# A planned transformer block on one core: all loads on one queue inside the plan, and the norm of segment 2 turned on TensorE

## The chip, the cores and the metric

The kernel runs on one core of a Trainium2 chip. The metric is device time in microseconds (us). A core has five engines that run side by side, each with a queue of its own in a fixed order: TensorE (PE), VectorE (DVE), ScalarE (ACT), GpSimd (POOL) and SyncE (SP). SP and ACT also issue DMA transfers[...].

## The reference

`x` has 2048 rows of 448, all in bf16. A vector `c` gives six modulation vectors through `silu(c) @ w_mod`.

```python
sa, ca, ga, sb, cb, gb = six rows of silu(c) @ w_mod
h = layernorm(x) * (1 + ca) + sa
x = x + ga * attention(h)          # 16 heads of 28, 4 segments of 512
h = layernorm(x) * (1 + cb) + sb
x = x + gb * ((sigmoid(h @ w_gate) * (h @ w_up)) @ w_down)   # inner width 1792
```

Attention is causal within a segment, with `g = sigmoid(beta)` for each head mixing in a memory of the earlier segments: `o = g * phi(q) M / (phi(q) z + 1e-6) + (1 - g) * softmax(q k) v`, and after each segment `M += phi(k)^T v`, `z += sum phi(k)`, with `phi(t) = t + 1` above zero and `exp(t)` below.

## The kernel before

**A plan, then the program.** The function builds a graph: `add` (L150) makes a node of each piece of work, with the engines that can do it, a duration, what it depends on and which buffers it takes. `Graph.run` (L209) plays this graph in planned time: each engine takes the ready node with the highest rank plus priority, where a choice of engine depends on `COST`, and PE stays with one kind of matmul for a bonus `STAY`. The order that comes out is written into each engine's queue. Small priorities for nearly all nodes stand in a table, `PRM`, by kind of work ("lg" logits, "ex" exponentials, "gu" gate and up, "mem" memory and so on). Planned times only decide the order; on the chip each engine goes through its queue in that order and waits where data is late.

**What is computed where.** A segment is 512 rows, four tiles of 128. For each segment:

- `ln1` (L792): statistics of a tile (L562, L563, DVE), 1/sigma (L569, L570, POOL), normalised tile `xn` (L575, DVE). Then `xn` has to be turned so that features lie on partitions (`hT`), and scale and shift are applied per partition. There are two ways. `turned` (L755) does it on PE: 32 transposes (L765) into four PSUM banks, then seven evacuations with scale and shift (L785 on DVE, L787 on ACT). The other way is four DMA transposes issued by SP (`transposed`, L708 and L710), then four modulations in place (`modulated`, L713; L720 ACT, L722 DVE or POOL), and two DMAs that copy halves of partitions (L727, L730). The tuple `PE_LN1` (L350) names the segments from the first on that take the PE way; segment 0 always does.
- `proj` (L813): q and k (L825) and v (L837) matmuls, evacuated by L808 (ACT) or L810 (DVE).
- `attention` (L887): logits (L906), exponentials (L920, L926, ACT), masks (L933 POOL, L936 DVE), values (`unit`, L953; L961), then small DVE work.
- `memory` (L856): phi of k (L850, L851, L853) gives `pq`, which a DMA transpose on SP (L861) turns to `pk`; the matmuls (L869) then add to the memory.
- `wo_ln2` (L1018): output projection (L1028), residual (L1031), second norm, turned by DMA for all segments.
- `ffn` (L1043): 14 chunks of gate and up (L1050), tanh (L1055, ACT), product (L1057, DVE), then the down projection (L1069), the residual (L1076) and the store (L1078).

All of PE's program order is one queue: a memory matmul that waits for its `pk` holds back every matmul placed behind it.

**The loads.** `load` (L438) makes a node of 600 ns on the issuing engine and a second node without work, released at a time `land` that is written by hand for each load. The plan takes the data to be there at that time. The transfers' sizes play no part, though `moved` (L171) and the queue clocks `self.ring` (L220) are in the code: no node passes `move`. A DMA transpose counts as landed 1240 ns after its issue (`lag`). The loads alternate: SP has `c`, tiles 0 and 2 of x, half of the first modulation weights, k weights, half of v and then most of the rest; ACT has tiles 1 and 3, the other half of the modulation weights, q weights, two tiles of segment 1, half of v, and both gate weights, the last behind segment 2's x. Their priorities `first(i)` (L468) follow the order of the source. The x of segment 3 (L673) waits for the warm-up matmuls (L657), which read its place. `scaled` (L699) multiplies each of the 14 chunks of down weights by `gb`; every chunk waits for all loads of down weights.

DMAs on SP share eight completion counters in turn, so a DMA waits until the eighth before it has landed.

```python
def load(eng, dst, src, land, deps=(), prio=0, use=(), take=()):
...
    n = add(eng, 600, fn, deps, prio=prio, use=use, take=take)
    return add("SP", 0, None, [n], prio=prio, release=land * 1000)
...
W_d = [scaled(wd_sb, k, 1, [n_gb, *l_wd]) for k in range(NFC)]
```

Of the kernel before, what the change touches and what calls it, by code (L numbers as in the profile page):

```python
# [13 lines left out]
P = 128  # L14
# [4 lines left out]
LAND = 1600  # L19
BACKLOG = 1500  # L20
INF = float("inf")
ALONE, SHARED = 215.0, 145.0

PRM = {
    "ws": (-1026557, -380405, -315274, -238661, -361567, 90434, -31526, -713703, -423901, -193540, 139595, 62071,
        -178802, 31458, -500017, -126626, -750922, -813085),
    "pj": (338550, 1240916, 411576, 1061850, 1037161, 271405, 605973, 841448, 517860, 274333, 556557, 602204, 435753,
        945539, 369290, 776037, 909231, 192884, 459168, 322714, 406428, 656300, 245224, -363562, -225384, -786626,
        -223846, -820139, -425637, -906561, -1127628, 367112, 198381, 481751, 18329, 758012, 1032656, 828671, 241536,
        -108484, 239872, -119492, 199009, -281816, 301267),  # L30
    "ev": (311356, 765090, 171478, 487831, 1411031, 758695, 745068, 1515510, 1532854, 1405197, 1664306, 1094315,
        -114560, 174326, 479074, -88836, 462561, 261587, 915583, 89350, 382455, 177146, -444871, 297079, -491875,
        -222386, -1021935, -1117245, -944968, -693323, -712045, 156181, -647130, -819253, -453667, -850771, 249532,
        470376, 69329, -181432, -477828, -275085, -331069, -936587, -284845, -325847, 8756, 195150),
    "ln1": (1117654, 765673, 978450, 1341531, 982229, 811634, 236741, 912635, 1047582, 168013, 717920, 598649, 902832,
        1278552, 1261149, 970655, 1361456, 978155, 746622, 409077, 386546, 264763, 501671, 55814, 137348, 244764,
        505320, 215607, 544820, 1205735, 581882, 756242, 340737, 854593, 668848, 969330, 981049, 750772, 802670,
        616966, 465825, 1027566, -527936, -40158, 551712, -96720, 326911, 50091, 727172, 256793, 1038149, -131304,
        434030, 588604, 808073, 645081, 880576, 1080680, 723034, 524922, 692343),
    "lg": (674902, 123695, 561301, 319397, 645874, 437068, 206227, 207503, 422863, 143555, 1405617, 879359, 868834,  # L40
        1242253, 807012, 1506890, 954487, 1724581, 1713292, 1378785, 1485021, 676801, 444818, 973580, 812305, 1769904,
        2086894, 2555751, 2316080, 3140941, 1912861, 1735115, 1765623, 1581983, 2149029, 1748985, 1870959, 2367380,
        1278299, 893760),
    "ex": (1061159, 1477133, 1739179, 1359130, 1621557, 896827, 896235, 802625, 1177741, 2146583, 883183, 786963,
        642153, 1848965, 1700468, 722258, 746990, 660348, 192999, 773605, 1217384, 1475898, 1178507, 1397622, 765939,
        582409, 211476, 196729, 217511, 138682, 267517, 735941, 973892, 608471, 890967, 881450, 1005686, 512596,
        717021, 1327086),
    "mask": (1520615, 1413694, 1279386, 2003105, 1818148, 1973568, 1670422, 2469718, 1732752, 2449207, 2306151,
        2540750, 2040307, 1834958, 2435499, 2237411, 1296838, 1432044, 1532957, 1218967, 1170467, 1705939, 960787,
        1030549, 742853, 1076535, 994933, 1817637, 1621845, 1174157, 1217475, 1346691, 104169, 318120, 14934, 89176,  # L50
        -135831, -486501, 272715, 347507, 378087, 1065118, -303844, 343822, 80679, -50290, -474178, -736840, -1557112,
        -1468651, -1261640, -1303527, -1057597, -1141215, -1062730, -1763005, -1399556, -1166602, -1202915, -1688388,
        -1993199, -1843840, -2304918, -2315887),
    "pv": (2080873, 874575, 1009647, 487727, 296192, 1097797, 857940, 480897, 821614, 1153384, 660808, 137298, 190263,
        216055, 377708, 836178),
    "t": (-44324, -21055, -29785, 323641, 1006485, 278236, 167569, 856460, 297038, 195779, 68830, 895442, 358856,
        455925, 730160, 976669, 660644, 556043, 354807, 376622, -321978, 157415, 864924, -137626, -13313, 290080,
        372271, 1258384, 607806, 1462055, 819535, 1127215, 1768030, 2069621, 812504, 1337124, 1749731, 1387778,
        1413501, 2478807, 2325887, 2562860, 1857402, 2208536, 2212781, 2183598, 2015299, 2167715, 598865, 1226474,
        520219, 548995, 636417, 958748, 460961, 506437, -81660, 79568, 966288, -7132, 344038, 633991, 435718, 626174,  # L60
        1339615, 932678, 1119918, 1241109, 965629, 1222800, 104675, 343254, 539346, 531196, 62549, -113912, 833029,
        813798, 408749, 253522, 741436, 740463, 767728, -6116, 485147, -287524, 95432, 156825, -74345, -203303,
        510344, 357634, 156656, -14091, -167467, 107793, -226537, -76689, 44264, -219803, 678406, 634786, 1038779,
        344264),
    "mem": (-185723, 115729, 59349, 101126, -27425, -125584, 150803, 226014, 77645, 95180, -386111, -12099, 159007,
        105014, -92900, 142903, -177695, -219275, 81591, 169437, 244125, -176994, 373563, 312329, 79103, 228949,
        339820, 303405, -105541, -4612, 38191, -535059, -581776, -270138, -483070, -69831, -419676, -163082, -119046,
        -338816, -647557, 205497, 121315, 18139, 1524, -617796, -58030, -28127, -466040, -307104, -92751, -96592,
        -453196, 116369, -188149, 204464, -251426, -250860, 458314, 392143, -371182, 9140, -889615, 673864, 781648,
        -240091, -16361, 399549, 206298, 47390, -303080, 370641, 102082, 458188, -136876, 332910, -790048, -209712,  # L70
        -550212, -485136, -241698, -185202, -576074, -371146),
    "wo": (2112408, 2093060, 2305611, 2035838, 435162, 1036304, 475885, 771414, 630045, 1079320, 1559197, 1122679,
        356509, 300181, -12581, -595879),
    "ln2": (1499349, 1911242, 2271005, 2227074, 1714614, 2066603, 2313937, 2292776, 2160756, 2211288, 2128912,
        2208921, 2494562, 2645243, 2017403, 2025602, 1875862, 2683834, 1770257, 1753157, 2151609, 1620369, 2211622,
        2044129, 2041746, 2243335, 561335, 696447, 969893, 837539, 590753, 252632, 1124331, 450641, 499934, 955682,
        653646, 594227, 565736, 929045, 685791, 706665, 954319, 503582, 1307997, 222097, 532639, 560506, 656449,
        953930, 865631, 662258, 747483, 724968, 974588, 920306, 1228076, 582694, 1487720, 1328136, 1048415, 948930,
        534287, 911788, 951510, 652778, 1847938, 1107426, 1049821, 668310, 1069501, 1109227, 1555135, 1261802,
        1318123, 2035851, 1417382, 2225008, -161015, 1031266, 1417875, 378351, 786858, 1716123, 1229095, 701535,  # L80
        769515, 857183, 963575, 521701, 391767, 1206676, 711474, 1156260, 880842, 923158, 606379, -147848, 528713,
        1255901, 447053, 717115, 872039, 365082),
    "gu": (982010, 1055412, 1188460, 953099, 705622, 838949, 1541378, 1520265, 1523761, 1634808, 949038, 1205958,
        832621, 1228260, 1311640, 290384, 877513, 536067, 481700, 502669, 400060, 885562, 705837, 515193, 270457,
        679260, 95423, 516376, 427829, 422138, -404887, -519560, 2520, -144327, 77521, -126967, 242348, -370325,
        -1248825, -108870, 41043, 293765, 182463, 2284, 520519, -709033, -533470, -308110, -919140, -1297023, -156020,
        -736908, -410023, -242206, -1116015, -657782, 472002, -58716, -30694, 26640),
    "tanh": (1916179, 1874612, 1112957, 1758741, 1844683, 2214238, 1662134, 1941088, 2051357, 2010608, 1710485,
        1638932, 1374883, 1611235, 657651, 874309, 137725, 129323, 697315, 1542469, 318956, 660289, 1212104, 668024,
        499705, 2746, 275789, -204972, -1127385, -525042, -1317983, -778761, -1052030, -953142, -1111022, -1480677,  # L90
        -247404, -561265, -648359, 340744, -871092, -628201, -599047, -491261, -651988, -197450, -489600, -495926,
# [18 lines left out]
STAY = 151782  # L110
# [1011 lines left out]
```

## Time and profile before

| | |
|---|---|
| median of 3 runs | 272.6 us (270.68 to 273.43) |
| the profiled execution | 274.04 us |
| its span, first to last instruction | 272.3 us |
| mean granted clock of TensorE | 0.937 |
| PE busy | 244.9 us (90%) |
| DVE busy | 194.0 us (71%) |
| ACT busy | 152.0 us (56%) |
| POOL busy | 48.9 us (18%) |
| read from HBM | 11.07 MB |

The profile's page cuts the span into 40 slices of 6.8 us, with the busy share of each engine in tenths, the clock granted to TensorE in tenths of the full one (PEclk) and the rate of the DMA engines (GB/s). Groups of instructions are named by line of the kernel, engine, and output and input by the program's names. A wait is written "engine line <- what released it: total us, times, longest". Times in a timeline count from the start of the span. Issue of a DMA is shown on its engine's queue (SPq).

### The profile page before, as it was taken

The page shows a single profiled execution, that of the slowest core. Times are in us where ns is not written, and L with a number is a line of the kernel's source. Part 1 is how long each engine was busy: PE and PEld are TensorE (multiplying, and loading weights), DVE is VectorE, ACT ScalarE, POOL GpSimd, SP SyncE. Part 2 cuts the span into 40 slices and gives each one's busy share as a digit, 9 for nine tenths or more (in the row PEclk, how much of TensorE's full clock was granted, in tenths as well). Part 3 has the DMA queues.
Part 4 walks back from the last instruction along what each step waited for, and adds up shares of the span by engine and source line. Part 5 has one row for each costly group of instructions (what it writes and reads, how often), then busy time and mean ns, then how long its engine had stood idle before and what let it go on. Part 6 is the DMA issues. An engine that isn't in the chain of part 4 may idle for free. (4 is left out here: it accounts for less than half of the span.)

```text
span 272.3 us, 5953 instructions
## 1 busy us (share of the span) xinstructions
PE 244.9 (90%) x2365; PEld 110.9 (41%) x2365; DVE 194.0 (71%) x484; ACT 152.0 (56%) x188; POOL 48.9 (18%) x104
## 2 busy tenths in 40 slices
PE   8799898187598798999998899989999999999995
PEld 3544653023243234443433543533444444445442
DVE  4579976296999979598898999759978653433431
ACT  2227979077979956466898589486621142112310
POOL 5204130041052001103501215303003110000000
PEclk9869899559999569999999999999999999999999
DMA  7999999930527510001035200240101320010001
GB/s 188 198 220 212 243 251 275 163 90 0 79 51 99 125 22 19 2 0 23 19 59 142 57 2 0 55 65 31 34 2 34 77 70 0 19 51 0 4 27 41
DMA packets 32103, 20.75 MB, mean 76 GB/s; under 512 B 20491, under 2 KB 30412, under 8 KB 32076
## 3 DMA queue, kind: packets, MB, share of 16 engines
q1 hardware_dynamic: 29868, 17.11, 30.4%
q10 hardware_dynamic: 2208, 3.27, 5.3%
q8 instruction: 18, 0.29, 0.5%
q14 instruction: 9, 0.07, 0.1%
HBM read 11.07 MB, written 1.84 MB: 47 GB/s over the span
## 5 line engine op out<-in xcount | busy, mean ns | idle before, releaser
L1050 PE MATMUL ps<-hT,wgu 64*128 64x512 bf16 x784 | 94.5, 385 | 2.3 <-DVE aT L810 0.9
L1055 ACT ACTIVATE tt<-ps 128x512 f32<-128x512 f32 x56 | 33.4, 597 | 66.6 <-PE ps L1050 65.8
L920 ACT ACTIVATE pT<-ps 128x2048 bf16<-128x2048 f32 x32 | 60.2, 1881 | 13.6 <-PE ps L906 11.9
L1057 DVE SCALAR_TENSOR_TENSOR fT<-tt,ps 128x512 bf16<-128x512 f32 x56 | 38.1, 682 | 31.7 <-ACT tt L1055 31.6
L1050 PEld LDWEIGHTS <-wgu 64*128 64x128 bf16 x784 | 40.2, 95 | 49.3 <-issue 13.1
L1069 PE MATMUL ps<-wd_sb,fT 128*128 128x448 bf16 x224 | 45.8, 353 | 0.2 <-DVE kT L810 0.2
L933 POOL TENSOR_SCALAR_AFFINE_SELECT pT<-pT 128x512 bf16<-128x512 bf16 x29 | 18.1, 635 | 73.1 <-DVE O L1009 21.1
L1069 PEld LDWEIGHTS <-fT 128*128 128x128 bf16 x224 | 20.4, 98 | 22.6 <-issue 5.7
L825 PE MATMUL ps<-hT,wqk 64*128 64x512 bf16 x224 | 28.8, 392 | 0.4 <-DVE x_sb L1031 0.4
L562 DVE BATCH_NORM_STATS2 st<-x_sb 128x6 f32<-128x448 bf16 x32 | 19.6, 614 | 3.0 <-DMA x_sb<-in_A_x_dram 2.5
L906 PE MATMUL ps<-qT,kT 28*128 28x512 bf16 (+3 forms) x256 | 17.0, 319 | 3.2 <-ACT pT L920 3.0
L825 PEld LDWEIGHTS <-wqk 64*128 64x128 bf16 x224 | 12.5, 97 | 14.0 <-issue 3.0
L926 ACT ACTIVATE pT<-ps 128x2048 bf16<-128x2048 f32 x8 | 15.0, 1875 | 5.2 <-PE ps L906 5.2
L1076 DVE TENSOR_TENSOR ot<-ps,x_sb 128x448 bf16<-128x448 f32 x16 | 9.8, 614 | 9.0 <-PE ps L1069 8.7
L570 POOL TENSOR_TENSOR rs<-rs,mhalf 128x1 f32<-128x1 f32 (+1 forms) x26 | 15.8, 609 | 2.2
L1028 PE MATMUL ps<-wo_sb,oT 128*128 128x448 bf16 x64 | 13.5, 353 | 2.5 <-ACT pT L920 1.5
L569 POOL TENSOR_SCALAR rs<-mv 128x1 f32<-128x1 f32 (+1 forms) x26 | 5.9, 227 | 54.0 <-DVE mv L563 51.7
L837 PE MATMUL ps<-wvv,hT 64*128 64x448 bf16 x112 | 14.7, 397 | 0.6 <-DMA hT<-hT 0.5
L936 DVE TENSOR_TENSOR pT<-pT,cmask 128x512 bf16<-128x512 bf16 x35 | 14.1, 425 | 1.3 <-ACT pT L920 1.3
L722 DVE TENSOR_SCALAR hT<-hT,cols 128x512 bf16<-128x512 bf16 (+1 forms) x19 | 6.5, 402 | 11.4 <-DMA hT<-xn 11.4
L961 PE MATMUL ps<-pT,vt 128*32 128x512 bf16 (+3 forms) x256 | 11.9, 304 | 1.7 <-DVE pT L936 1.1
L575 DVE TENSOR_SCALAR xn<-x_sb,mv,rs 128x448 bf16<-128x448 bf16 x32 | 11.4, 400 | 1.5 <-POOL rs L570 1.5
(95 smaller groups left out, 243.0 us busy)
## 6 DMA issues: line engine op xcount, KB each, us to landing
out_dram<-ot SPq DMA_DIRECT2D x16, 112.0 KB, 1.7
hT<-hT SPq DMA_DIRECT2D x6, 256.0 KB, 3.2
hT<-hT SPq DMA_DIRECT2D x6, 192.0 KB, 3.4
x_sb<-in_A_x_dram SPq DMA_DIRECT2D x2, 448.0 KB, 11.9
wgu<-in_B_w_up_dram SPq DMA_DIRECT2D x1, 896.0 KB, 13.6
wgu<-in_B_w_gate_dram ACTq DMA_DIRECT2D x1, 896.0 KB
wd_sb<-in_B_w_down_dram SPq DMA_DIRECT2D x2, 448.0 KB, 16.5
fT<-in_w_mod_dram SPq DMA_DIRECT2D x2, 392.0 KB, 11.9
```

Source lines behind the costliest of these rows:

```text
L562: nc.vector.bn_stats(st_r[:, st.at, :], src)
L570: nc.gpsimd.tensor_tensor(r, r, mhalf[:, 0:w], ALU.pow)
L825: nc.tensor.matmul(pf(b), lhsT=w, rhs=piece(hT, i, half), start=(i == 0), stop=(i == NP - 1))
L837: nc.tensor.matmul(pf(b)[:, 0:D], lhsT=piece(hT, i, half)[:, (t + half) * P:(t + half + 1) * P], rhs=wvv[half * HR:(half + 1) * HR, chunk_ ...
L906: nc.tensor.matmul(ps[:, lg.at + hs, o:o + nq], lhsT=kT_r[r, k.at, hcs[u], kb * P:(kb + 1) * P], rhs=qT_r[r, q.at, hcs[u], kb * P:L], star ...
L920: nc.scalar.activation(pT_r[:, pTs[units[0]].at, :, w0:w0 + L], ps_, AF.Exp, scale=scale)
L926: nc.scalar.activation(dst, ps_.rearrange("p h (u w) -> p u h w", u=2), AF.Exp, scale=scale)
L933: nc.gpsimd.affine_select(out=blk, in_=blk, compare_op=ALU.is_ge, fill=0.0, base=0, pattern=[[0, 4], [1, P]], channel_multiplier=-1)
L1050: nc.tensor.matmul(pf(b), lhsT=wgu[half * HR:(half + 1) * HR, chunk_of(i, half), fs], rhs=piece(hT, i, half), start=(i == 0), stop=(i == N ...
L1055: a = act(485, lambda gp=gp, tt=tt: nc.scalar.activation(tt_r[:, tt.at, :], pf(gp), AF.Tanh, scale=0.5), [n], use=[gp, tt], prio=pr("tanh" ...
L1057: f = dve(597, lambda up=up, tt=tt, ft=ft: nc.vector.scalar_tensor_tensor(fT_r[:, ft.at, :], tt_r[:, tt.at, :], 1.0, pf(up), op0=ALU.add, ...
L1069: nc.tensor.matmul(pf(b)[:, 0:D], lhsT=fT_r[:, fts[fc].at, t * P:(t + 1) * P], rhs=wd_sb[:, fc, :], start=(fc == 0), stop=(fc == NFC - 1))
```

## The change

- Every load becomes one node whose landing the plan works out from its size: `move=size` puts it on a queue clock (`moved`) that gives one queue 245 bytes per ns alone and 128 when both move. `LAND` (800) is added, and a load over 100,000 bytes is planned once its queue has under `BACKLOG` (4000 ns) ahead. DMA transposes and the two shifting DMAs go on the same clock as 60,000 and 80,000 bytes.
- Behind the first modulation weights all loads are issued by SP; ACT keeps two tiles of x and half of the first modulation weights. Gate and up weights come in four parts each rather than two. The later loads get priorities from the table (kind "ld").
- A chunk of down weights waits for its own load only (`l_wd[k]`).
- `PE_LN1` becomes (1, 2): segment 2's first norm is turned on PE.
- All values of `PRM`, `STAY` and `COST` are others, so the order of nearly all work is new.

In the order that is built, SP issues x0, c, x2, half of the first modulation weights, q, k, beta, x4-5, x6-7, v, the third modulation part, x8-11, the fourth and fifth, the four of the output weights, up 0-1 and 2-3, gate 0-1 and 2-3, up 4-5, x12-15, up 6, down 0-3; then the memory's first transpose, a down part, the second transpose, the sixth modulation part, a down part, the third transpose, gate 4-5 and 6, the last down part, the fourth transpose.

```diff
-LAND = 1600
-BACKLOG = 1500
+LAND = 800
+BACKLOG = 4000
-ALONE, SHARED = 215.0, 145.0
+ALONE, SHARED = 245.0, 128.0
...
-STAY = 151782
-COST = {"ACT": 1.037, "DVE": 1.012, "POOL": 0.764}
+STAY = 85343
+COST = {"ACT": 1.117, "DVE": 1.247, "POOL": 0.77}
...
-        self.ring = {"SP": 0.0, "ACT": 0.0}
+        self.ring = {"SP": 800.0, "ACT": 800.0}
...
-                        n.lag = self.moved(e, n.end, n.move) - n.end + LAND
+                        n.lag += self.moved(e, n.end, n.move) - n.end + LAND
...
-    PE_LN1, PE_LN2 = (1,), ()
+    PE_LN1, PE_LN2 = (1, 2), ()
...
-        n = add(eng, 600, fn, deps, prio=prio, use=use, take=take)
-        return add("SP", 0, None, [n], prio=prio, release=land * 1000)
+        return add(eng, 450 if size < 200000 else 640, fn, deps, prio=prio, use=use, take=take, move=size, lag=300)
...
+    load_wm(("ACT", "SP"), 0, 2, pT_r[:].rearrange("p n h w -> p (n h w)"), first(5))
+    W_qk = [load_half("SP", wqk_st, half, w, first(6 + half)) for half, w in enumerate((A_wq, A_wk))]
+    load_x("SP", TPS, TPS + 2, first(8))
+    load_x("SP", TPS + 2, 2 * TPS, first(9))
+    W_v = [load_half("SP", wvv, i, A_wv, first(10 + i)) for i in range(2)]
...
+    W_gu = [load_half("SP", wgu, half, w, ld(), c0, c1) for c0, c1 in ((0, 2), (2, 4), (4, 6), (6, 7))
+            for half, w in ((0, B_w_gate), (1, B_w_up))]
+    load_x("SP", 3 * TPS, 4 * TPS, ld(), [n_warm, n_pads, *n_vpad, *n_vone, *n_opad])
+    load_wm(("SP",), 5, 1, fT_flat[:, 3 * NK * D:], ld())
+    l_wd = []
+    for f0, f1 in ((0, 4), (4, 7), (7, 11), (11, 14)):
+        l_wd += [load("SP", wd_sb[:, f0:f1, :], B_w_down.rearrange("(fc p) n -> p fc n", p=P)[:, f0:f1, :],
+                      (f1 - f0) * P * D * 2, W_p if f0 < NC else (), prio=ld())] * (f1 - f0)
...
-    W_d = [scaled(wd_sb, k, 1, [n_gb, *l_wd]) for k in range(NFC)]
+    W_d = [scaled(wd_sb, k, 1, [n_gb, l_wd[k]]) for k in range(NFC)]
...
-        return add("SP", 1305, fn, [n], use=[xn, hT], prio=prio, lag=1240)
+        return add("SP", 1305, fn, [n], use=[xn, hT], prio=prio, move=60000)
```

## The prediction

> **What bounds the kernel now.** I read the page's 40 slices first, then the busy time by stretches, then the waits of TensorE (PE), then the timeline around the longest of them. The slices and the stretches show two different kernels.
>
> ```profile
> PE   8799898187598798999998899989999999999995
> ...
> DVE  4579976296999979598898999759978653433431
> ...
> PEclk9869899559999569999999999999999999999999
> ...
> GB/s 188 198 220 212 243 251 275 163 90 0 79 51 99 125 22 19 2 0 23 19 59 142 57 2 0 55 65 31 34 2 34 77 70 0 19 51 0 4 27 41
> ```
>
> A slice is 6.8 us. From slice 15 (about 100 us) PE is full and its clock whole. Before that PE has holes and four stretches of lowered clock, the deepest hole in slice 8. The GB/s row falls from 275 to 90 there: the loads end where the hole is.
>
> ```profile
> 46.50:53.35 6.85, 0.00 (x0) 0.00 (x0) 0.58 (x2) 1.34 (x3) 0.00 (x0) 0.67 1.16 201
> 53.35:63.50 10.15, 9.06 (x88) 3.29 (x92) 8.12 (x26) 6.05 (x7) 4.69 (x7) 0.55 0.32 73
> 63.50:97.12 33.62, 25.59 (x312) 10.72 (x306) 31.84 (x94) 29.63 (x34) 6.38 (x12) 0.89 0.41 72
> 97.12:272.30 175.18, 167.27 (x1534) 74.10 (x1530) 119.94 (x263) 87.89 (x106) 26.10 (x50) 0.99 0.14 33
> ```
>
> Columns: length, busy time of PE, PE weight loads, DVE, ACT, POOL, then clock, DMA share, GB/s. From 97.12, the first tanh of the feed-forward, PE sets the end (167.3 of 175.2 us). From 63.5 to 97 DVE (31.8 of 33.6) and ACT (29.6) set the pace. From 46.5 to 53.35 nobody works.
>
> ```profile
> PE ps L869 <- DMA pk<-pq: 7.8, 3, 6.9
> ```
> ```profile
> 44.11 6.61 SPq L710 DMA_TRANSPOSE hT<-xn  x4
> ...
> 50.81 2.53 SPq L861 DMA_TRANSPOSE pk<-pq  x2
> 52.77 1.37 DVE L722 TENSOR_SCALAR hT<-hT,cols 128x512 bf16<-128x512 bf16 x4 [7.21 <-DMA hT<-xn]
> 53.35 0.30 PE L869 MATMUL ps<-vt,pk 128*32 128x32 bf16 x16 [6.88 <-DMA pk<-pq]
> ...
> 54.65 1.88 ACT L920 ACTIVATE pT<-ps 128x2048 bf16<-128x2048 f32 x1 [6.81 <-PE ps L906]
> ```
>
> The reader is to see one jam with three victims. SP issues in order; the four DMA transposes of segment 2's norm start only at 44.11, behind the loads, and take 6.61 us to issue; the memory's transposes (pk) follow at 50.81. PE's queue stands at the memory matmul (L869), so the next logits are not issued and ACT stands 6.81 us; DVE waits 7.21 us for hT. All three lose the same time, so all of it is on the path.
>
> **The change part by part.** Only the order in which each engine's instructions were placed is read from the changed code; every duration is from this profile.
>
> *Norm of segment 2.* Removed: four DMA transposes and two shifting DMAs on SP, four modulations (3 on DVE by this trace's 0.34 us pitch, 1.0 us; one on POOL). Added: 32 PE transposes at 0.061 us (32 took 1.96 us at 27.6), 2.0 us; seven PSUM evacuations, five on DVE at 0.49 (2.45 us) and two on ACT at 0.78 (1.55 us). PE has the room before 97 us (25.6 of 33.6 busy), so its 2.0 us cost nothing there; without that cover they would cost 2.0.
>
> *The jam.* In the new SP order the first pk transpose follows loads of 8.83 MB, the second 9.17 MB, no hT transpose before either (before: all 11.07 MB and four transposes). The GB/s of five-us stretches add up to 8.5 MB at 39 us and 9.17 MB at 42.2. Issue of the transpose ahead 1.19, issue to landing 2.5: the second lands at 42.2 + 1.2 + 2.5 = 45.9. When does PE ask? It now has eight logits groups, not six, ahead of that matmul. ACT's list to the end of the seventh exp is 25.5 us from its first evacuation; it needed 27.7 us for 26.2 in this trace, so 27.0, from 19.5: 46.5. DVE makes the second pq at about 41.5 (cumulative 31.2 us, against 31.4 at 41.6 here). So the wait of 6.9 shrinks to something between 0 and 3; I take 1.0. What is late next: the loads held back on SP while it waits for pq (2.24 MB: the last modulation weights, gate and down weights). They are then due by about 53; PE asks for the modulation weights (second `rep`) near 57 and for all gate weights near 88. Covered, by 10 us or more for the first once its own 1.8 us are counted from about 43.
>
> *Start.* On the ACT queue nothing now follows the first modulation weights, on SP the other loads do. Here the halves released PE at 8.65 and 9.81; both by 8.65 would be 1.1 earlier, but the six warm-up matmuls ahead of the first projection (2.45 us at the low clock) stay. Bounds 0 to 1.1; I take 0.7: projections from 17.3. The q and k weights, now in sequence on one queue, land at 2.06 MB, some 11.5, ahead of the 14.8 at which DVE got them here. The weights for L614's second pair land at 4.99 MB, 24.7 plus about 2, asked for near 28: no stall, 1 us to spare. ACT loses its two issues of gate loads (about 0.9 us), not counted as busy.
>
> *The sum to the first tanh.* DVE: the two instruction lists up to the first L1057, group by group, differ by −2.9 us (five masks fewer −2.0, six down-weight scalings fewer −2.3, three output-weight scalings more +1.2, hT +2.45 −1.0, memory work moved behind −1.5, evacuation +0.7, rest −0.4). Busy from 17.96 to 97.12 was 64.75, so idle 14.4, of it 6.3 in the jam. New: 61.9 + 14.4 − 6.3 + 1.0 = 71.0, from 17.3: 88.3. ACT: busy 58.9 from 20.14 to 97.12, idle 18.1, of it 6.8 the jam; its list grows by 0.8 (two hT more, one copy fewer): 59.7 + 18.1 − 6.8 + 1.0 = 72.0, from 19.4: 91.4. Some of ACT's other idle time is waiting for PE at half clock behind the jam, which goes with it, so I take 90.0: 7.1 us earlier than 97.12.
>
> *After it.* The PE lists behind the first 28 gate/up matmuls are equal, 164.2 us in both at full-clock pitches (0.112 per gate/up matmul, 0.198 down, 0.1155 q/k, 0.105 v, 0.2025 output projection, 0.66 per attention unit). Here they took 175.2; the 11 us over are waits and slow clock. The interleaving is new everywhere (all priorities changed), which can move those 11 by −2 to +6; I take 0, as the work is the same and DVE and ACT have no more of it. Where DVE scales fewer weights, POOL does more before: it is 18% busy.
>
> *A rule against a row.* The Trainium skill, "TensorE: Matmul & The Clock Gate", Part 1, has the clock halve after an idle window of about 3.4 us. By it, without the jam the clock would stay whole from 20 us on. The row differs: the clock fell to 0.50 from 89.9 to 100 (PE busy 8.8 us) after no gap over 1.1 us, and from 31.9 to 35. So I keep both dips. By the rule another 4.4 + 1.5 us would be won: 259.6; by the row 265.5. A rule that speaks against the change: "DMA: Bandwidth & Descriptors", on queues and rings, has each DMA engine alternate between queues, so loads on a second queue do not stand ahead of SP's transposes. The 0.92 MB of gate weights now ahead of pk (about 4 us) could have been there; by the rule pk lands near 42, by the row near 46, where PE asks: worth 0 to 1 us, inside my 1.0.
>
> The profiled execution took 274.04 us: 272.3 span and 1.7 around it. Its span would be 272.3 − 7.1 = 265.2. It is 1.4 over the median of the runs, so the saving is taken from the median: 272.6 − 7.1 = **265.5**.
>
> **Rivals.**
> (1) *One queue moves less than two* (the other side). The pk transposes then land late and the jam returns in full, with DVE's last hT evacuation behind the memory copies that wait for them. The wait is 2 + 9.17/r + 3.7 − 46.5. At r = 195 GB/s it is 8.1 and eats all of the gain; at 185 it is 10.8 and the time 275.3; at 170, 279.6. For: 207 GB/s in 17 to 24 us, where by bytes only SP's queue had work, is near. Against: 218 in 37 to 44, also SP alone, 216 with both from 5 to 17, and 273 where the long-row gate and up weights moved. Time 279.
> (2) *The gain is given back later.* PE's 11 us over its list grow by 3 to 6, since PE's order meets DVE, which is 84% busy from 100 to 200 us, at new places. For: waits of 0.4, 0.9 and 1.2 on DVE at 105, 151 and 181 already. Against: same work, and attention moved forward. 270.
> (3) *The clock dips go too*, as the rule has it; the warm-up pairs now spread between 24 and 31 us speak for the first dip, DVE-bound work at 63 to 97 against the second. 260.
>
> **How the numbers follow.** Forecast 0.53 (own range 262 to 268.5), rival 1 0.16, rival 2 0.19, rival 3 0.12. About 1% (2.7 us) is what a measurement of this kernel tells from no change: faster is below 269.9, slower above 275.3. Faster: 0.53 + 0.12 + 0.08 of rival 2 = 0.73. Same: 0.11 of rival 2 and 0.01 of rival 1 = 0.12. Slower: 0.15. The range from 258.5, a little under rival 3, to 276, the near end of rival 1, leaves out some 0.04 below and 0.14 above.
>
> **What would show it.** Right: no wait of PE for pk over 3 us near 45; first tanh at 87 to 92; clock whole from 36 to about 80; GB/s near 220 with SP's queue alone; 175 us from first tanh to the end. Wrong: loads still running at 50; a wait for weights at the second `rep`; a first tanh before 92 but an end after 270 (rival 2).

## The result and the profile after

| | before | after |
|---|---|---|
| median, in the same comparison | 271.85 us (270.68 to 273.43) | 263.94 us (263.5 to 264.54) |
| the profiled execution | 274.04 us | 264.14 us |
| its span | 272.3 us | 262.3 us |
| start of the first q and k projections | 17.96 | 18.16 |
| first tanh of the feed-forward | 97.12 | 89.38 |
| from there to the end | 175.18 | 172.92 |
| mean granted clock | 0.937 | 0.961 |

The ratio is 0.9707 [0.9647, 0.9767]. The two spans differ by 10.0 us and the medians by 7.9: the profiled execution of before was 2.2 us over its median, so some 2 us of what the two profiles show between them is spread. In the changed kernel the line numbers are higher for the same statement, from L676 of before on by 8 (the memory's transpose is L861 before and L869 after, its matmul L869 and L877). The experiments' kernels are numbered differently again; there it is best to go by the names. The slices of the page of after, in the order of those shown of before:

```profile
PE   8699887799996899989989999999999999999994
...
DVE  3568799969899879899799999869985443433431
...
PEclk9869999679999599999999999999999999999999
...
GB/s 159 221 217 188 199 224 171 290 111 72 13 111 90 64 0 23 0 63 62 72 45 0 57 35 37 27 92 0 20 25 95 84 0 2 35 35 4 0 35 37
```

A slice is now 6.6 us. The hole of slice 8 is gone from PE's row and DVE's; PE's thinnest places are slices 2, 7, 8 and 13. Three stretches of lowered clock are left (slices 2 and 3, 8 and 9, and 14), where before had four. DMA traffic at a high rate goes on to 55 us, through the place of the old jam.

The stretches that answer to those shown of before, by columns: length, busy time of PE, PE weight loads, DVE, ACT, POOL, then clock, DMA share, GB/s.

```profile
44.50:46.91 2.41, 0.03 (x3) 0.05 (x2) 2.27 (x8) 2.41 (x3) 0.30 (x1) 1.00 0.99 169
46.91:55.00 8.09, 7.57 (x82) 3.23 (x83) 6.19 (x19) 5.71 (x6) 2.55 (x4) 0.59 1.11 265
...
80.00:89.38 9.38, 5.78 (x88) 2.23 (x86) 9.24 (x26) 7.89 (x8) 2.06 (x2) 0.81 0.42 94
18.16:89.38 71.22, 62.55 (x743) 27.28 (x744) 64.14 (x187) 58.92 (x68) 20.91 (x40) 0.93 0.75 146
89.38:262.30 172.92, 166.77 (x1534) 73.00 (x1530) 120.10 (x270) 89.35 (x110) 27.39 (x48) 0.99 0.15 34
```

From the projections to the first tanh the kernel before took 79.16 us with DVE busy for 64.75. Now it is 71.22 with 64.14: DVE has nearly as much to do, and stands still for 7.1 us in place of 14.4. The 6.3 us that DVE stood in the jam are most of that difference. The place of the old jam (first line) has PE idle still, for 2.4 us, but DVE and ACT are full there. The timeline of after around it, filtered here to the lines that matter:

```profile
41.60 0.42 DVE L861 TENSOR_TENSOR pq<-e 128x512 bf16<-128x512 bf16 x1
...
42.13 1.84 SPq L869 DMA_TRANSPOSE pk<-pq  x1
...
44.02 1.37 SPq L443 DMA_DIRECT2D fT<-in_w_mod_dram  x1
...
45.52 0.43 DVE L861 TENSOR_TENSOR pq<-e 128x512 bf16<-128x512 bf16 x1
45.86 1.44 DVE L793 TENSOR_SCALAR hT<-ps,cols 128x512 bf16<-128x512 bf16 x3
...
46.91 0.83 PE L773 MATMUL ps<-ident,xn 128*128 128x128 bf16 x12 [2.38 <-DVE hT L793]
...
48.00 0.40 PE L877 MATMUL ps<-vt,pk 128*32 128x32 bf16 x32
```

The memory matmul (L877) runs at 48.00 with no wait for pk on record here (the longest one left, 2.1 us, stands at 83.3, at the next segment's memory). PE waits before it, in the turned norm: the transposes of L773 need a PSUM bank that DVE's evacuation (L793) has not emptied, and DVE comes to that evacuation late, behind statistics and phi of k. Under that wait lies another. The second pk transpose goes out at 42.13, 0.1 us after its pq is made (41.60 + 0.42 = 42.02), but by the trace it lands 5.9 us later, at 48.1 (the first, out at 40.11, after 6.5, at 46.6); two transposes of the kernel before with no loads left in flight (50.81 and 52.08) landed about 2.5 us after issue. So pk is there just when PE, held up by the norm, comes to it.

### The profile page after: what moved, and what is told of

Same layout as the page of the kernel before. It is cut to its first block, busy times and chain, and to the rows that moved or that the text cites. A ratio compares the mean times of both kernels' runs of the same rounds, so it can differ in the third digit from the quotient of the medians.

```text
span 262.3 us, 6017 instructions
## 1 busy us (share of the span) xinstructions
PE 244.1 (93%) x2397; PEld 108.3 (41%) x2397; DVE 192.7 (73%) x482; ACT 153.6 (59%) x192; POOL 53.6 (20%) x111
## 4 chain that ended last, share of the span: by engine, by line
PE 54%; DVE 6%; DMA 5%; ACT 1%; POOL 1%; issue 1%; POOLq 0%; SPq 0%; DVEq 0%; ACTq 0%
PE ps L1058 30%; PE ps L1077 15%; DMA hT<-hT 2%; PE ps L833 2%; PE ps L914 2%; PE ps L969 2%; PE ps L1036 2%; DMA pk<-pq 1%; DMA hT<-xn 1%; DVE fT L1065 1%; DVE ot L1084 1%; DVE hT L730 1%; DVE x_sb L1039 1%; ACT pT L928 1%; PE ps L984 1%
## 5 line engine op out<-in xcount | busy, mean ns | idle before, releaser
L1058 PE MATMUL ps<-hT,wgu 64*128 64x512 bf16 x784 | 93.3, 384 | 1.4 <-DMA hT<-hT 0.9
L1058 PEld LDWEIGHTS <-wgu 64*128 64x128 bf16 x784 | 38.7, 95 | 49.9 <-issue 12.7
L1077 PE MATMUL ps<-wd_sb,fT 128*128 128x448 bf16 x224 | 45.1, 353 | 0.0
L941 POOL TENSOR_SCALAR_AFFINE_SELECT pT<-pT 128x512 bf16<-128x512 bf16 x25 | 15.8, 636 | 62.1 <-ACT pT L928 26.6
L914 PE MATMUL ps<-qT,kT 28*128 28x512 bf16 (+3 forms) x256 | 16.4, 311 | 1.3 <-ACT pT L928 1.2
L944 DVE TENSOR_TENSOR pT<-pT,cmask 128x512 bf16<-128x512 bf16 x39 | 15.9, 428 | 2.3 <-ACT pT L928 2.3
L576 POOL TENSOR_TENSOR rs<-rs,mhalf 128x1 f32<-128x1 f32 (+1 forms) x29 | 17.0, 588 | 2.4
L833 PEld LDWEIGHTS <-wqk 64*128 64x128 bf16 x224 | 10.9, 96 | 14.5 <-issue 4.2
L709 POOL TENSOR_TENSOR wd_sb<-wd_sb,rep 128x448 bf16<-128x448 bf16 x10 | 10.3, 1032 | 23.9 <-DVE rm L890 8.3
L845 PE MATMUL ps<-wvv,hT 64*128 64x448 bf16 x112 | 13.2, 373 | 0.4 <-DVE qT L818 0.4
```

The costliest lines, as they stand in the source:

```text
L576: nc.gpsimd.tensor_tensor(r, r, mhalf[:, 0:w], ALU.pow)
L833: nc.tensor.matmul(pf(b), lhsT=w, rhs=piece(hT, i, half), start=(i == 0), stop=(i == NP - 1))
L914: nc.tensor.matmul(ps[:, lg.at + hs, o:o + nq], lhsT=kT_r[r, k.at, hcs[u], kb * P:(kb + 1) * P], rhs=qT_r[r, q.at, hcs[u], kb * P:L], star ...
L944: nc.vector.tensor_tensor(blk, blk, cmask[:].rearrange("p (o k) -> p o k", o=1).to_broadcast([P, 4, P]), ALU.mult)
L1058: nc.tensor.matmul(pf(b), lhsT=wgu[half * HR:(half + 1) * HR, chunk_of(i, half), fs], rhs=piece(hT, i, half), start=(i == 0), stop=(i == N ...
L1077: nc.tensor.matmul(pf(b)[:, 0:D], lhsT=fT_r[:, fts[fc].at, t * P:(t + 1) * P], rhs=wd_sb[:, fc, :], start=(fc == 0), stop=(fc == NFC - 1))
```

## The experiments

Three theories. **Q**: what stood ahead of the memory's transposes on SP's queue made the jam, and holding loads back behind them is the gain. **N**: the norm of segment 2 had to leave the DMA queue. **S**: only the new order everywhere brings it.

**e1, the kernel before with the memory's transposes first.** SP's order alone is edited, after planning: pk, pk, the four hT transposes of segment 2, then the sixth modulation part and segment 3's x (`late`), and the four down-weight loads (`down`) behind the two copies of halves. In the kernel before all of these loads stood ahead of the transposes. A load's tag is its planned landing time.

```diff
+        pk = [order[tags.index(("pk", 0, i))] for i in (0, 1)]
+        hT = [n for n in order if n.tag == ("hT",)][0:4]
+        late = [n for n in order if n.tag and n.tag[0] == "load" and n.tag[1] in (39, 41, 45, 46, 47, 48)]
...
+        down, late = late[2:], late[0:2]
+        moving = pk + hT + late
...
+        order[i:i] = moving
```

> The kernel before with the compute order of every engine kept; only SP's queue is in another order: the memory's first two transposes stand directly behind the up weights, then segment 2's four norm transposes, the sixth modulation part, x of segment 3, and the four down-weight loads behind the norm's shifting copies. Theory Q (what was ahead of the transposes on SP's queue made the jam, and moving it is the gain): the wait of PE for pk near 46 us falls from 6.9 to under 2, segment 2's norm is turned by 48 rather than 52.8, and the time is 264 to 267. Rival N (the norm of segment 2 has to leave the DMA queue): the jam moves from pk to hT, which is still turned by DMA, half of the gain, 267 to 269. Rival S (the new order of the work everywhere is the gain, the queue only a part of it): 269 to 272.

Measured: 270.8 us (270.05 to 271.77), ratio 0.9956 [0.9925, 0.9987]. The wait for pk at 46 went; another of the same size came. From the waits between 40 and 60 us:

```profile
PE ps L652 <- DMA fT<-in_w_mod_dram: 7.0, 1, 7.0
...
DVE hT L743 <- DMA hT<-xn: 5.6, 1, 5.6
```

PE stood 7.0 us for the sixth modulation part, which my edit had put behind the transposes. So it tells nothing about Q's size, and led to e5.

**e5, the same with the sixth modulation part left ahead.**

```diff
+        late = [n for n in order if n.tag and n.tag[0] == "load" and n.tag[1] in (41, 45, 46, 47, 48)]
...
+        down, late = late[1:], late[0:1]
```

> The kernel before with its own order of compute on every engine; on SP's queue alone, the memory's first two transposes go ahead of segment 2's four transposes, of the last four loads of segments 2 and 3 of x, and of the down weights; unlike in the run before it, the sixth part of the modulation weights stays ahead of them (0.39 MB, some 1.8 us at the rate of loads seen there). Theory Q (what stood ahead of the memory's transposes on SP's queue made the jam): the wait for pk at 46 stays under 1.5 us, the wait of 7.0 us for the sixth modulation part is gone, first tanh at 88 to 92, time 264 to 267.5. Theory N (the norm of segment 2 had to leave the DMA queue): its four transposes now come later still, DVE waits for hT as before, first tanh at 95 to 97, time 270 to 273. Theory S (only the new order everywhere brings the gain): the first tanh comes at 88 to 92 but 180 us or more follow it, time 270 to 273.

Measured: 271.4 us (270.15 to 272.4), ratio 0.9941 [0.9907, 0.9975]; span 269.3, first tanh at 95.08. Its timeline:

```profile
44.83 5.88 SPq L729 DMA_TRANSPOSE hT<-xn  x4
...
46.63 0.27 PE L894 MATMUL ps<-vt,pk 128*32 128x32 bf16 x16
...
52.07 1.37 DVE L743 TENSOR_SCALAR hT<-hT,cols 128x512 bf16<-128x512 bf16 x4 [6.28 <-DMA hT<-xn]
...
55.86 4.53 PE L860 MATMUL ps<-wvv,hT 64*128 64x448 bf16 x23 [5.36 <-DVE M_sb L901]
```

The memory runs on time at 46.63. But the four norm transposes still begin at 44.8 and take 5.9 us to issue. DVE's queue stands at the modulation for 6.28 us (7.21 before), and PE's v projection waits 5.36 us for a copy of the memory (M_sb) that is queued on DVE behind it. This is what N expected of this run; Q's 264 to 267.5 is missed by 4 us. Freeing one of the two victims moves the time by 0.6%: the other had been hidden behind it. The edit itself put pk ahead of the norm's transposes, though: their inputs `xn` are written at 37.7 to 40.6, before pq is. SP's order with the norm's transposes first, pk next and the held loads behind both was not tried, so whether the order of SP's queue alone could bring the gain stays open.

**e2, the norm alone.** The kernel before with segment 2 turned on PE; the norm's table entries for segment 2 are segment 1's, shifted by a constant, and the plan made anew.

```diff
...
-    PE_LN1, PE_LN2 = (1,), ()
+    PE_LN1, PE_LN2 = (1, 2), ()
```

> The kernel before with segment 2's norm turned on PE and the loads as before (the plan is made anew, with segment 1's norm priorities moved for segment 2). Theory Q: all 11.07 MB of loads still stand ahead of pk, but four transposes (6.6 us of issue) do not: pk lands near 51 rather than 53.3 and the jam is 3 to 5 us; 268 to 271. Rival N: the jam goes, 264 to 267. Rival S: an order that was not searched for loses more than it gains, 272 to 277.

Measured: 288.0 us (287.06 to 289.47), ratio 1.0575 [1.0499, 1.0651]; first tanh at 101.89. PE's waits:

```profile
PE ps L804 <- DMA pk<-pq: 9.4, 3, 8.5
```

Without the norm's transposes on SP the wait for pk stays at 8.5 us: PE asks earlier, at 40.6, and goes on at 49.07, where before it went on at 53.35. The norm alone does not dissolve the jam. The time itself is that of an order whose priorities fit another graph: 183.4 us follow the first tanh, 8 more than before.

**e4, the loads alone.** The changed kernel with segment 2's norm on the DMA queue again; its table entries are segment 3's, shifted, and the plan made anew.

```diff
...
-    PE_LN1, PE_LN2 = (1, 2), ()
+    PE_LN1, PE_LN2 = (1,), ()
```

> The changed kernel with segment 2's norm turned by DMA transposes again (planned anew, with segment 3's norm priorities moved for segment 2). Theory Q: the plan knows the queue and places pk early, so most of the gain stays: 264 to 267. Rival N: the four transposes and two copies go back on SP among the loads and the jam is back: 270 to 273. Rival S: the new table no longer fits its plan, 267 to 272, with small waits everywhere and none over 3 us.

Measured: 286.24 us (285.11 to 288.59), ratio 1.0517 [1.0424, 1.0609]. The first tanh comes at 90.47, 1.1 us after that of the changed kernel; the longest wait for pk is 1.2 us. SP's queue shows how:

```profile
36.83 6.47 SPq L651 DMA_TRANSPOSE hT<-xn  x4
43.36 1.13 SPq L376 DMA_DIRECT2D wd_sb<-in_B_w_down_dram  x2
```

With loads in the plan by size, the four transposes are placed at 36.83, ahead of the down weights, and the longest wait for them is 1.7 us (ACT, at 45.5) where it had been 7.2 (DVE). So the jam can go with this norm on the DMA queue. That the front part as a whole is as short is not shown: by its first tanh e4 has done less, as 8.1 us more of PE's busy time and 3.0 of ACT's lie behind it than in the changed kernel. Then 192.9 us follow to the end (172.9 after): PE is busy 174.9 us of them and idle 18. That part of the loss was not traced further; the table, searched for another graph, is the likely cause, and that is argued, not shown.

**e3, the held loads ahead again.** The changed kernel with the six loads that it holds back (2.24 MB) issued ahead of the first pk transpose; nothing else differs.

```diff
+        i = order.index(next(n for n in order if n.tag == ("pk", 0, 0)))
+        late = [n for n in order[i:] if n.tag == ("load",)]
+        rest = [n for n in order if n not in late]
+        i = rest.index(next(n for n in rest if n.tag == ("pk", 0, 0)))
+        order = rest[0:i] + late + rest[i:]
```

> The changed kernel with every engine's compute order kept; on SP's queue the six loads that stood between and behind the memory's first transposes (2.24 MB) now stand ahead of them. Theory Q: the second pk lands near 54 (11.07 MB at the 200 GB/s of this kernel, plus 2.5) while PE asks at 48, so a wait of 5 to 7 us with a lowered clock behind it is back: 269 to 272. Rivals N and S: segment 2's norm is on PE and the order is the new one, so nothing changes by more than 1 us: 263 to 265.

Measured: 270.32 us (268.97 to 273.31), ratio to before 0.9943 [0.9898, 0.9988]; 6.4 us more than the changed kernel. SP's queue, then PE:

```profile
42.49 0.59 SPq L450 DMA_DIRECT2D wd_sb<-in_B_w_down_dram  x1
43.18 16.46 SPq L878 DMA_TRANSPOSE pk<-pq  x4
```
```profile
53.87 0.30 PE L888 MATMUL ps<-vt,pk 128*32 128x32 bf16 x16 [8.28 <-DMA pk<-pq]
```

(The transposes' row runs from the first issue to the end of the fourth.) The jam is back at its place and larger than in the kernel before; from the projections to the first tanh it is 78.1 us now, where the changed kernel has 71.2. The norm is on PE and the order new on every other engine, and of the 7.9 us gained, 6.4 are gone. Within the changed kernel Q is shown.

**e7, two queues of loads.** The changed kernel with gate 0-3 (0.9 MB) issued by ACT at the same place in the order.

```diff
-            (nc.sync if eng == "SP" else nc.scalar).dma_start(dst, src)
+            (nc.sync if (q or eng) == "SP" else nc.scalar).dma_start(dst, src)
...
+    W_gu = [load_half("SP", wgu, half, w, ld(), c0, c1, "ACT" if half == 0 and c0 < 4 else None) for c0, c1 in ((0, 2), (2, 4), (4, 6), (6, 7))
```

> The changed kernel; the two loads of the gate weights' first four columns (0.9 MB) are issued from ACT's queue at the place that they have in the order, all else the same: two queues of loads instead of one. If one queue moves less than two: the GB/s of 20 to 40 us add up to 5% more, the loads end 1 to 3 us earlier, the memory's transposes on SP are issued up to 4 us earlier; but no wait for them is left at 46, so the time stays within 1 us of the changed kernel's 263.9. If the bytes ahead decide whatever the queue: the same GB/s, the transposes at 40 and 42 us as in the changed kernel, time 263.5 to 265. If ACT's issue of two loads is paid for on ACT: up to 1.3 us more.

Measured: 263.32 us (261.0 to 263.73), ratio to before 0.9639 [0.9588, 0.969]. GB/s of five-us stretches, from the start of the span:

| | 15-20 | 20-25 | 25-30 | 30-35 | 35-40 |
|---|---|---|---|---|---|
| before | 208 | 209 | 215 | 273 | 250 |
| after | 219 | 184 | 191 | 226 | 207 |
| e6 (loads as in after) | 223 | 213 | 203 | 213 | 224 |
| e3 (all loads ahead) | 231 | 236 | 209 | 218 | 221 |
| e7 (gate 0-3 on ACT's queue) | 226 | 221 | 210 | 215 | 208 |

From 15 to 30 us ACT's queue moves next to nothing in any of them (0.02 of 3.16 MB before, none in e7), so there it is one queue everywhere, and the low 184 and 191 of after are the spread of single executions: the others have 203 to 236. From 30 on two queues move in the kernel before (ACT's 1.51 of 2.61 MB up to 40 us) and in e7 (0.91 of 1.88 MB up to 39). e7 is no faster there with two queues than after, e6 and e3 are with one. Only the kernel before is faster at 30 to 40; its gate and up weights move in halves of 896 and 672 KB, where the changed kernel's move in parts of 448 and 224 KB. Whether the smaller parts are the cause was not tried. SP's queue in e7 shows what 0.9 MB less ahead of pk on its queue bring:

```profile
40.44 1.31 SPq L869 DMA_TRANSPOSE pk<-pq  x1
...
42.48 1.20 SPq L869 DMA_TRANSPOSE pk<-pq  x1
```

Nothing. They go out as their pq is made, as in the changed kernel, and land 6.1 and 5.5 us later, at 46.5 and 48.0, against 46.6 and 48.1 there. The gate bytes on ACT's queue had moved by 39 us, though, before pk went out, and had slowed SP's loads meanwhile. What pk would do beside loads still in flight on the other queue is not tested by this.

**e8, q weights on ACT's queue.**

```diff
-    W_qk = [load_half("SP", wqk_st, half, w, first(6 + half)) for half, w in enumerate((A_wq, A_wk))]
+    W_qk = [load_half("SP", wqk_st, half, w, first(6 + half), q="ACT" if half == 0 else None) for half, w in enumerate((A_wq, A_wk))]
```

> The changed kernel; the q weights (0.39 MB) are issued from ACT's queue, behind the first modulation weights, all else the same. Between 3 and 6 us the changed kernel's DMA share is only 0.61 to 0.77, and its second half of the first modulation weights lets TensorE go on at 9.95 us. If one queue does not put enough in flight there: DMA share 0.9 or more from 3 to 6, the wait for the first modulation weights no longer, projections at 17.2 to 18.2, time 263 to 264. If a second queue only takes bandwidth from the modulation weights: that wait grows by 0.4 to 1.0 us and with it the first projection (18.5 to 19.2), time 264 to 265.

Measured: 263.03 us (261.56 to 264.05), ratio to before 0.9632 [0.9575, 0.9689]. The DMA share from 3 to 6 us rises to 0.86, yet PE waits for the first modulation weights until 10.10. With start loads exactly as in after that was 9.05 (e3), 9.95 (after), 10.18 (e7) and 10.47 (e6). So one execution says this time only to some 1.4 us, and e8 is inside that: inconclusive; its median is 0.3 us below that of e7. The second pk lands at 46.0 in e8, 2.1 us before that of after, and the turned norm still waits 2.4 us for DVE.

**e6, TensorE kept busy at 81 to 86.** Of the second disputed number, the clock.

```diff
             def mm(hc=hc, pk=pk, b=b):
+                for _ in range({0: 8, 1: 5}.get(hc, 0) if s == 1 else 0):
+                    nc.tensor.matmul(pf(b), lhsT=ident[:], rhs=wqk[:, 0, :, :].rearrange("p h e -> p (h e)"), start=True, stop=True)
                 for kb in range(TPS):
```

> The changed kernel with 13 extra matmuls of 512 columns (8 and 5) into the memory's own PSUM bank, overwritten after them, ahead of segment 1's memory matmuls at about 81 to 86, where TensorE is 36 to 53% busy and where its clock then falls to 0.5 from 86 to 93. They add work and no result. If the clock falls there because TensorE was too idle in the 5 us before: the clock stays at 0.9 or more from 86 to 93, the feed-forward's first 24 matmuls take some 2.5 us less, and the time is 261 to 263. If the clock falls for another cause (what TensorE does before makes no difference): the granted clock stays near 0.5 somewhere in 84 to 95 and the time is 264 to 266, the extra matmuls costing up to 2 us.

Measured: 261.3 us (260.17 to 264.05), ratio to before 0.9594 [0.9546, 0.9641]: the lowest median of all. By stretches, the changed kernel first, then e6:

```profile
80.00:83.00 3.00, 1.08 (x24) 0.48 (x20) 3.00 (x8) 3.00 (x4) 1.03 (x1) 1.00 0.45 92
83.00:86.00 3.00, 1.58 (x46) 0.76 (x47) 2.93 (x9) 3.00 (x4) 0.51 (x1) 0.98 0.54 111
86.00:89.00 3.00, 2.73 (x16) 0.82 (x17) 2.93 (x11) 1.89 (x2) 0.51 (x1) 0.50 0.31 92
89.00:93.00 4.00, 4.00 (x24) 1.29 (x24) 1.59 (x5) 1.74 (x4) 1.66 (x2) 0.54 0.00 0
```
```profile
80.00:83.00 3.00, 2.46 (x36) 0.89 (x34) 2.93 (x9) 2.92 (x4) 0.70 (x1) 1.00 0.43 87
83.00:86.00 3.00, 2.39 (x33) 0.88 (x32) 2.56 (x10) 2.40 (x2) 1.03 (x1) 1.00 0.63 154
86.00:89.00 3.00, 1.53 (x15) 0.72 (x15) 1.97 (x6) 1.37 (x3) 0.64 (x1) 1.00 0.02 4
89.00:93.00 4.00, 4.00 (x50) 1.72 (x48) 3.37 (x9) 3.35 (x5) 1.04 (x1) 1.00 0.00 0
```

PE's busy share at 80 to 86 goes from 2.66 of 6 us to 4.85, and the clock then stays whole: from 89 to 93, 50 matmuls and not 24 fit into the same 4 us. First tanh at 88.50, 170.6 us from there. The runs agree: the mean granted clock is 0.967 to 0.980 in five of the six (0.961 in the slowest, 264.05 us), and 0.954 to 0.966 in all twelve of after, e7 and e8. So PE's low activity had lowered the clock here, and work that nobody needs, put where PE would stand anyway, keeps it up. What it is worth in time is less sure. Set beside the changed kernel by their ratios to before, 0.9594 / 0.9707 = 0.988, 1.2% less, with some 0.8% of doubt from the two intervals; set beside e7 and e8, which were measured together with it and differ from the changed kernel in one queue each, it is 0.7 to 0.8%, and the ranges of the runs overlap. The same filling for the start, where PE stands 2 to 4 us from 6.4 us on and the clock is 0.50 from 11 to 16, was not tried.

## Why the prediction was right, step by step

The end was right: 265.5 forecast, 263.94 measured, inside its own range; a saving of 7.1 us forecast, 7.9 measured. The reason given, loads ahead of pk, holds too (e3). That the first tanh came as near as 89.38 to the 90.0 forecast is in part luck: errors met. For DVE the sum was 17.3 + 61.9 + 9.1 = 88.3; measured, 18.16 + 64.14 + 7.08 = 89.38.

- **Start, 0.7 us: not gained.** Both halves were to be there by 8.65. PE waited until 9.95, and 9.05 to 10.47 in three other kernels with the same start. The 1.1 us between 8.65 and 9.81 was the spread of single executions, read as an effect.
- **The jam, 6.9 to 1.0: right in kind, wrong in what is left.** No wait for pk shows at this place. What I had as late next were the loads, and they are not late: the second `rep` does not wait. Late next is the norm that was moved: its transposes wait 2.4 us for DVE (2.4 in e3, e6, e7 and e8 as well), and 0.5 us follow at M_sb. I had costed it as 2.0 us of PE time with room and 4 us of evacuations, and did not ask when DVE comes to them. For DVE, which sets the pace, the jam is gone to 0.14 us of idle time, better than the 1.0 assumed.
- **pk lands at 45.9: it landed at 48.1.** The step took the loads' rate of before, which brought 9.17 MB from 2 to 42.2 us (228 GB/s), and after moved 210 GB/s in that time, 8.4 MB. Part of this is spread: e6, e7 and e3, which issue the same loads up to there, moved 219, 216 and 226, and the second pk landed at 47.1 in e6, 48.0 in e7 and 46.0 in e8 (whether from e8's edit is not known). PE was to ask at 46.5; without the norm's wait it would have come to the memory 2.4 us before 48.0, at 45.6. So in this execution a wait for pk of up to 2.4 lay hidden under the norm's; in e8, by the same working, none did.
- **DVE's list, −2.9: only −0.6 showed** (64.75 to 64.14 busy). From the start of the span to the first product the instructions do add up to 2.9 us less. But the sum needed them from the projections to the first tanh, and there the difference is −1.3: before had two masks between its first tanh and its first product, and 0.7 of what is saved lies ahead of the projections. The rest, 0.7, is overlap of the recorded times, which busy time counts once. In return DVE's idle time outside the jam fell by 1.2 us, where the sum had kept it.
- **No stall at L614's second pair: 0.9 us.** The "1 us to spare" was used up in this execution (wait for fT at 30.2); e6, e7 and e8 show no such wait.
- **After the first tanh, 0: −2.3.** PE busy 167.3 to 166.8, idle 7.9 to 6.1. The new order has shorter waits there, and this is more than spread: e1 and e5, with before's order, have 174.8 and 174.2 us, e3, e7 and e8, with after's, 172.9, 172.6 and 173.4. The bounds of −2 to +6 were a little tight.
- **Both dips kept: the row held, the rule did not.** The rule taken from the Trainium skill, "TensorE: Matmul & The Clock Gate", Part 1, an idle window of about 3.4 us, would have the clock whole from 20 us. It fell at 48 behind a gap of 2.4 us, and from 86 behind a stretch whose longest gaps were 2.1 and 1.2 us. One dip of the two, at 31 to 35, did go; that the spread warm-up pairs did it is not shown. **Rival 3**, both dips gone at 260, so came true by half. e6 prices the other dip: its stretch behind the first tanh is 2.3 us shorter.
- **The rule on queues, 0 to 1 us: 0.** In e7 the gate weights on the second queue move the landings of pk by 0.1 us at most. The rule itself (the Trainium skill, "DMA: Bandwidth & Descriptors", on queues and rings) was not put to the test, as those weights had moved before pk went out.
- **Rival 1** (one queue slower) did not come true. Its sums are off: by its own formula the wait is 6.2 us at 195 GB/s, not 8.1, and the gain is eaten at 188. Its "218 in 37 to 44, also SP alone" is misread too: ACT's queue moved 0.61 of those 1.53 MB. The kernels with one queue moved 210 to 226 GB/s from 2 to 42 us, and e7 was no faster with two.
- **Rival 2** (given back later) did not happen with the priorities that came with the change. It did in e4 and e2, whose first tanh says little about their end.

Q was first stated too simply. In the order of before, two users of SP's queue sit in one jam, and freeing either alone (e2: pk waits 8.5; e5: hT waits 6.3) leaves the other. What the change does is put both ahead of need, one by holding loads back and one by leaving the queue. For the first, e3 shows the worth. For the second, e4 shows that both can be in time on the DMA queue, with another order; so the norm on PE is one way and not shown to be needed.

## What to carry to other kernels

When several engines wait for one in-order DMA queue, list each user behind the blockage with the time at which it would be asked for; freeing the longest wait alone only shows the next (e5), and 2.24 MB of weights needed late are worth 6.4 us when they stand ahead of a small transpose that is needed now (e3). A time from a single profiled execution is known no better than it repeats (1.4 us at this start, 1.0 for the landing of pk in after and e6), so no gain smaller than that is to be read from one row. Ahead of a stretch that is bound by TensorE, look at its clock and at how busy it was just before: 13 wasted matmuls kept the clock whole here and may be worth 0.7 to 1.2% (e6).

## What was not expected of the hardware

The granted clock falls after low activity that is no single long gap: at 80 to 86 PE was busy 2.66 us of 6, longest gap 2.1 us, and the clock was 0.50 from 86 to 89. It also falls on a grid. In the trace of after it changes at 10.76, 17.59, 48.31, 55.13, 85.85 and 92.68, always a multiple of 3.41 us apart. The stretches between these times, and the 3.41 us ahead of each fall, by the same columns:

```profile
7.35:10.76 3.41, 1.18 (x23) 0.69 (x22) 1.50 (x7) 0.00 (x0) 1.43 (x3) 1.00 1.13 228
10.76:17.59 6.83, 6.83 (x83) 4.63 (x82) 3.81 (x11) 1.17 (x3) 0.00 (x0) 0.50 1.14 218
44.89:48.31 3.42, 1.40 (x52) 1.07 (x51) 3.25 (x10) 3.02 (x5) 0.82 (x2) 1.00 1.07 225
48.31:55.13 6.82, 6.30 (x46) 2.17 (x32) 4.83 (x16) 4.76 (x5) 1.73 (x3) 0.50 1.09 258
82.44:85.85 3.41, 1.58 (x46) 0.76 (x47) 3.34 (x10) 3.41 (x4) 0.43 (x2) 1.00 0.51 106
85.85:92.68 6.83, 6.41 (x34) 1.99 (x33) 4.67 (x14) 3.46 (x5) 2.33 (x3) 0.50 0.15 43
```

PE was busy for 1.18, 1.40 and 1.58 of 3.41 us ahead of the three falls. This makes sense of two things that look odd. At the start PE stood from 7.7 to 9.9 and worked again, and the clock fell only at 10.76, the next step of the grid. In e6 a thin place of about 3 us (85 to 88, busy 0.92 of 3.00) lowered nothing: it lies across a step, and the 3.41 us on either side (83.08 to 86.49 to 89.90) were busy for 2.50 and 2.24. No threshold comes out of these traces: in the kernel before the clock fell at 31.71 behind 3.42 us with PE busy for 2.79, and held behind two with 1.95 (69.25 to 76.08).
